# A gated scan with mixture-of-experts: expert weights loaded on another DMA queue, and a new order of the first chunk

## The chip, the cores and the metric

One Trainium2 chip, one core. The metric is the device time of one execution in microseconds; lower is better. TensorE does the matmuls, VectorE and ScalarE the elementwise work, POOL (GpSimd) issues indirect transfers from its own queue, and SP (SyncE) issues plain transfers from another.

## The reference

A gated scan over 4 sequences of 5056 tokens with 256 channels makes h; then every token is given to one of 8 experts, greedily in the order of its logits, at most 2528 tokens to each; each expert is a two-layer network.

```python
sig = 1.0 / (1.0 + np.exp(-f_logit))
f = lower_bound + (1.0 - lower_bound) * sig
h = f[:, t] * h + (1.0 - f[:, t]) * x[:, t]        # for every t; y[:, t] = h
logits = y.reshape(N, 256) @ w_gate                 # N = 20224, 8 experts
...                                                 # greedy: best logit first, cap N // 8
out[mask] = np.maximum(y[mask] @ w1[e], 0.0) @ w2[e]   # w1[e] 256 x 1024, w2[e] 1024 x 256
```

## The kernel before, in words

Up to about 165 us the kernel runs the scan, chunk by chunk, and writes the rows of h to a DRAM buffer, `hbuf`; SP issues the loads and these stores. A search over thresholds (functions `search`, `assign`, `compact`) then finds the expert that fills first, its tokens, and the row numbers of these tokens. The order in which experts come is known only at run time, so the index of the weights in use, the tile `wi`, is computed by VectorE.

From there the function `moe` runs expert after expert. An expert k has 20 blocks of 128 tokens, in chunks of up to four blocks; expert 0's first chunk has two. A chunk c has eight steps j, one for each 128 columns of the hidden layer. Each float32 operand is split into a high part in fp32r and a low part, the remainder, and each product is three matmuls: high by high, high by low, low by high.

- `load_w` (line 1050) puts the loads of expert k's weights, w1 in two halves of 512 KB and w2, at the head of the list `issues`; each is an indirect transfer on POOL that reads its row numbers from `wi`. `issue` (1039) pops from that list; in the main loop one transfer is issued per step, each waiting for the evacuation named last in `gate`. For expert 0, w2 comes in two halves, which lines 1406 to 1412 place on POOL behind the first chunk's gathers.
- `split` (1074) cuts the raw weights into eight pieces: 0 to 3 are w1, of 512 columns (pieces 0 and 1 serve steps 0 to 3 for the two halves of the contraction, 2 and 3 steps 4 to 7), 4 to 7 are w2, for two steps each. `high` writes a piece's high part on ScalarE (tiles w1h, w2s), `low` its low part on VectorE (w1l, w2s). For expert 0 the list `RAMP` (1071) says which pieces are done at each tick of `sp0`, four ticks before the first step and one after the matmuls of each step.
- `gather` (1122) lists the indirect loads of a block's rows (tile xg); `trans` (1168) transposes them on TensorE, and ScalarE and VectorE write the high and low parts xh and xl.
- `first` (1198) is one step of the first layer: six matmuls into a bank of the pool `pws` (three buffers, tile pw), which ScalarE evacuates to hh and VectorE to hl. These evacuations are not emitted at once but kept as `posts`; `flush` (1153) emits those that a model of the engines' time holds for ready, and with an argument all those up to that step.
- `second` (1263) is one step of the second layer, into tile py. `first_lag` (1431) says how many steps of the second layer have been emitted by the end of steps 3, 4 and 5; afterwards it is two steps behind.
- `tick` (1440) emits background work: the routing of later experts, the rest of the row numbers, and the split of the next expert's weights. As long as `sp0` is not done it does nothing but `flush`.

The order on TensorE, VectorE and ScalarE is the order of emission; the queues of POOL and SP are ordered by the framework. Filler matmuls (tile bz) run on TensorE while it waits for the search.

```python
    for i in range(len(todo) + LAG):
        step = i
        flush(i - 2 if i < len(todo) else i)
        ...
            first(k, c, j)
            if not sp0.done:
                flush()
            sp0.tick(True)
            tick()
        ...
        while made < first_lag.get(i, i - LAG + 1):
            second(*todo[made])
```

Of the kernel before, what the change touches and what calls it, by code (L numbers as in the profile page):

```python
# [1002 lines left out]
def moe(ctx, tc, g):  # L1003
    pace = g["pace"]
    nc = Paced(tc.nc, pace)
# [42 lines left out]
        return st  # L1048

    def load_w(k, layers=(1, 2)):  # L1050
        def load(dst, src, n):
            return lambda: nc.gpsimd.indirect_dma_start(out=dst, out_offset=None, in_=src,
                                                        in_offset=off(WI[k][:, n:n + 1]))
        rows = []
        r1 = r2 = None
        if 1 in layers:
            r1 = wraw.tile([P, 2, F], F32, name="r1")
            rows = [load(r1[:, 0], w1v, 0), load(r1[:, 1], w1v, 1)]
        if 2 in layers:
            r2 = wraw2.tile([P, FB, D], F32, name="r2")  # L1060
        if 2 not in layers:
            pass
        elif k:
            rows.append(load(r2.rearrange("p j d -> p (j d)"), w2v, 2))
        else:
            rows += [load(r2[:, s * FB // 2:(s + 1) * FB // 2].rearrange("p j d -> p (j d)"), w2u, 3 + s)
                     for s in range(2)]
        issues[:0] = [(("w", k), x) for x in rows]
        RAW[k] = r1 or RAW[k][0], r2

    RAMP = [((0, 1), (0,)), ((2,), (1,)), ((3,), (2,)), ((), (3,)), ((4,), ()), ((5,), (4,)), ((6,), (5,)),
            ((7,), (6,)), ((), (7,))]

    def split(k):
        if k:
            issue(upto=lambda what: what == ("w", k))
        r1, r2 = RAW[k]
        w1h = wsp.tile([P, 2, FB, P], F32R, name="w1h")
        w1l = wsp.tile([P, 2, FB, P], F32R, name="w1l")
        w2s = wsp.tile([P, FB, 2, 2, P], F32R, name="w2s")  # L1080
        WS[k] = w1h, w1l, w2s
        pieces = []
        for j0, h in ((0, 0), (0, 1), (4, 0), (4, 1)):
            src = r1[:, h].rearrange("p (q j) -> p j q", j=FB)[:, j0:j0 + 4]
            pieces.append((src, w1h[:, h, j0:j0 + 4], w1l[:, h, j0:j0 + 4], omlb[:, h:h + 1]))
        for j0 in range(0, FB, 2):
            src = r2[:, j0:j0 + 2].rearrange("p j (b a) -> p j a b", a=2)
            pieces.append((src, w2s[:, j0:j0 + 2, :, 0], w2s[:, j0:j0 + 2, :, 1], None))
        def high(n):
            src, hi, lo, scale = pieces[n]  # L1090
            if scale is None:
                nc.scalar.activation(hi, src, AF.Copy)
            else:
                nc.scalar.activation(hi, src, AF.Identity, scale=scale)

        def low(n):
            src, hi, lo, scale = pieces[n]
            if scale is None:
                v.tensor_sub(lo, src, hi.bitcast(F32))
            else:  # L1100
                v.scalar_tensor_tensor(lo, src, scale, hi.bitcast(F32), op0=OP.mult, op1=OP.subtract)

        steps = RAMP if k == 0 else [((n,), (n - 1,)) for n in range(len(pieces) + 1)]
        for i, (hs, ls) in enumerate(steps):
            prog[k]["left"] = len(steps) - i
            for n in hs:
                if n < len(pieces):
                    high(n)
            for n in ls:
                if n >= 0:  # L1110
                    low(n)
            yield 'ACT',

    def tiles(k, c):
        b, n = CHUNKS[k][c]
# [49 lines left out]
    def woven(t):  # L1165
        return t.rearrange("p a b -> p b a")

    def trans(k, c, h, now=False):
        ns = tiles(k, c)
        w, m = sum(ns), 2 if len(ns) <= 2 else 1  # L1170
        if h == 0:
            issue(upto=lambda what: what == ("g", k, c))
            XS[k, c] = (xp.tile([P, 2, 512], F32R, name="xh"), xp.tile([P, 2, 512], F32R, name="xl"))
        elif m == 2:
            return
        xh, xl = (turn2(t)[:, h:h + m, :, :w // 2] for t in XS[k, c])
        if now:
            def part(q):
                pt = pws.tile([P, 512], F32R, name="pw")
                pt = pt[:, :2 * P].rearrange("p (m w) -> p m w", m=2)  # L1180
                for i in range(2):
                    nc.tensor.transpose(pt[:, i], XG[k, c][:, q, i * P:(i + 1) * P], ident_r)
                pt = pairs(pt.bitcast(F32))
                qh, ql = (t[:, :, :, q * P // 2:(q + 1) * P // 2] for t in (xh, xl))
                up = post("ACT", (pt,), lambda: nc.scalar.activation(qh, pt, AF.Copy), None, now)
                post("DVE", (xh,), lambda: v.tensor_tensor(ql, pt, qh.bitcast(F32), op=OP.subtract), up, now)
                g["busy"](g["WARM"][q], g["RA"])
            return [part(q) for q in range(2)]
        pt = pws.tile([P, 512], F32R, name="pw").rearrange("p (m w) -> p m w", m=m)
        for q, n in enumerate(ns):  # L1190
            for i in range(m):
                nc.tensor.transpose(pt[:, i, q * P:q * P + n], XG[k, c][:n, q, (h + i) * P:(h + i + 1) * P],
                                    ident_r[:n, :n])
        pt = pairs(pt.bitcast(F32)[:, :, :w])
        up = post("ACT", (pt,), lambda: nc.scalar.activation(xh, pt, AF.Copy), None, now)
        return post("DVE", (xh,), lambda: v.tensor_tensor(xl, pt, xh.bitcast(F32), op=OP.subtract), up, now)
# [191 lines left out]

    main.until(lambda: have(0, "wi"))
    load_w(0, (1,))  # L1390
    issue(2)
    main.until(lambda: 0 in comp)
    for _ in g["kept"]:
        pass
# [4 lines left out]
    gp = ctx.enter_context(tc.tile_pool(name="gp", bufs=3))  # L1399
    wraw2 = ctx.enter_context(tc.tile_pool(name="wraw2", bufs=1))  # L1400
    load_w(0, (2,))
    wsp = ctx.enter_context(tc.tile_pool(name="wsp", bufs=2))
    xp = ctx.enter_context(tc.tile_pool(name="xp", bufs=2))
    hp = ctx.enter_context(tc.tile_pool(name="hp", bufs=FB))
    yp = ctx.enter_context(tc.tile_pool(name="yp", bufs=YB))
    halves = [issues.pop(0)[1] for _ in range(2)]
    gather(0, 0)
    rows = issue(99)
    for half in halves:
        tc.add_manual_dep(half().ins, rows.ins.name,  # L1410
                          mybir.DependencyInfo(mybir.DependencyClass.NoSync, mybir.DependencyReason.SCHED_ONLY),
                          reason="rows first")
    gather(0, 1, (0, 2))
    issue(99)
    comp[0].tick(True)
    comp[0].tick(True)
    sp0 = Bg(split(0))
    sp0.tick(True)
    gather(0, 1, (2, 4))
    gather(0, 2, (0, 1))  # L1420
    issue(99)
    sp0.tick(True)
    trans(0, 0, 0, True)
    sp0.tick(True)
    sp0.tick(True)
    sp = None
    todo = [(k, c, j) for k in range(E) for c in range(len(CHUNKS[k])) for j in range(FB)]
    starts = {kk: n for n, (kk, cc, jj) in enumerate(todo) if (cc, jj) == (0, 0)}
    order = [(k, c) for k in range(E) for c in range(len(CHUNKS[k]))]
    gathers = order[2:]  # L1430
    first_lag = {3: 0, 4: 1, 5: 2}
    made = 0
    LAG = 3
    wn = 1
# [4 lines left out]

    def tick():  # L1440
        nonlocal sp, wn
        if not sp0.done:
            return flush()
        if not any(rows_due(q) and comp[q].tick() for q in (k, k + 1)):
            main.tick()
        flush()
        for q in (k, k + 1, k + 2):
            if q in comp and not comp[q].done:
                comp[q].tick()
        if sp is None:  # L1450
            if wn == k + 1 and wn < E and have(wn, "wi"):
                load_w(wn)
                sp = Bg(split(wn), WAITS)
                sp.wait = WAITW
                wn += 1
        elif not sp.done:

            sp.tick(within=max(0, starts[k + 1] - i - 1) * 6 / prog[k + 1].get("left", 9))
# [4 lines that stand above are left out]
        if i < len(todo):  # L1463
            k, c, j = todo[i]
            if (c, j) == (0, 0) and k:
                assert wn == k + 1
                sp.until(lambda: sp.done)
                sp = None
            first(k, c, j)
            if not sp0.done:  # L1470
                flush()
            sp0.tick(True)
            tick()
            NS = len(CHUNKS[k])
            if gathers:

                kk, cc = gathers[0]
                ahead = order.index((kk, cc)) - order.index((k, c))
                if ahead == 1 and j >= 1 or ahead == 2 and j >= (2 if (k, c) == (0, 0) else 0) and have(
                        kk, "ids", sum(CHUNKS[kk][cc])):  # L1480
                    gather(kk, cc, (1, 4) if (kk, cc) == (0, 2) else None, soon=ahead == 1 or c == len(CHUNKS[k]) - 2 and j > 0)
                    gathers.pop(0)
            at = T0 if k < 2 and c in (0, NS - 1) else TJ
            nxt = order.index((k, c)) + 1
            if j in at and nxt < len(order):
                trans(*order[nxt], at.index(j))
# [35 lines left out]
```

## Time and profile before

| | |
|---|---|
| median of 3 runs | 1106.17 us (1104.99 to 1108.45) |
| the profiled execution | 1104.47 us, of which the span of instructions is 1102.7 us |
| granted clock of TensorE | 0.999 of full speed |
| busy, of the span | TensorE 98%, VectorE 73%, ScalarE 48%, POOL 40% |
| DMA | 121.76 MB, 58.22 on POOL's queue and 62.14 on SP's |
| chain that ended last | TensorE 80% |

All times in the profile count from the start of the span. PE is TensorE, PEld its loading of weights, DVE is VectorE, ACT is ScalarE; a q behind the name means its queue of instructions. In a timeline a row gives the start, the length, the engine, the operation with its output and inputs, their shapes, and how many such instructions the row merges; in brackets stand the engine's idle time before it and what ended it. The tile r stands for r1 and r2, the raw weights, and also for a small tile of the routing; the operation tells them apart. L109 is a helper through which most operations pass.

### The profile page before, as it was taken

The numbers are of one execution on the slowest core, as the hardware profiler recorded it, in microseconds if no ns is written. First come the engines' busy times: TensorE is split into PE (matmuls) and PEld (weight loads), VectorE is DVE, ScalarE is ACT, GpSimd is POOL, SyncE is SP. The second block draws the span as 40 slices with busy tenths as digits, with TensorE's granted clock in tenths as the row PEclk, the third lists the DMA queues.
The fourth block names the chain that finished last, engine by engine and source line by source line (L and its number), as shares of the span: only waits on it lengthen the run. The fifth ranks groups of instructions, "written<-read, shape, count | busy, mean of one in ns | idle before, by whom it ended". The sixth has DMA issues, their size and how long they took to land.

```text
span 1102.7 us, 21642 instructions
## 1 busy us (share of the span) xinstructions
PE 1084.4 (98%) x8230; PEld 959.9 (87%) x8230; DVE 803.4 (73%) x2048; ACT 533.6 (48%) x1223; POOL 446.0 (40%) x428
## 2 busy tenths in 40 slices
PE   8999998999999999999999999999999999999998
PEld 6888787999988898888888888888888888898897
DVE  7999878878877896789778877887787664334333
ACT  7999775332733454245424642264226573323322
POOL 6787404332533343344333333433343433333332
PEclk9999999999999999999999999999999999999999
DMA  9999894112111311131113111311113221111110
GB/s 372 410 399 376 318 362 140 54 38 96 63 48 44 114 50 43 43 119 58 44 44 114 48 45 46 111 57 44 48 57 109 96 73 50 49 49 52 48 48 38
DMA packets 36493, 121.76 MB, mean 110 GB/s; under 512 B 7714, under 2 KB 7716, under 8 KB 35492
## 3 DMA queue, kind: packets, MB, share of 16 engines
q0 software_dynamic: 18960, 58.22, 15.6%
q1 hardware_dynamic: 17424, 62.14, 14.6%
q8 instruction: 65, 1.06, 0.4%
q14 instruction: 40, 0.33, 0.1%
q10 hardware_dynamic: 4, 0.00, 0.0%
HBM read 78.91 MB, written 41.42 MB: 109 GB/s over the span
## 4 chain that ended last, share of the span: by engine, by line
PE 80%; issue 1%; DMA 1%; DVE 1%; POOL 0%; ACT 0%; POOLq 0%; ACTq 0%
PE pw L109 38%; PE py L109 37%; PE rt L109 4%; DMA r<-in_moe_w_dram,wi 1%; POOL out_dram L109 0%; POOL r L109 0%; DVE hl L109 0%; DVE w2s L109 0%; ACT y L109 0%; POOLq L1518 0%; DVE w1l L109 0%; ACT hh L109 0%; DVE asg L109 0%; DVE y L109 0%; DVE g L109 0%
## 5 line engine op out<-in xcount | busy, mean ns | idle before, releaser
L109 PE MATMUL py<-w2s,hh 128*128 128x512 f32 (+3 forms) x1448 | 453.4, 366 | 0.0
L109 ACT ACTIVATE hh<-pw 128x512 fp32r<-128x512 f32 (+3 forms) x336 | 192.0, 572 | 436.5 <-PE pw L109 399.0
L109 PE MATMUL py<-w2s,hl 128*128 128x256 f32 (+1 forms) x1280 | 349.6, 273 | 0.0
L109 DVE SCALAR_TENSOR_TENSOR hl<-pw,hh 128x512 fp32r<-128x512 f32 (+3 forms) x336 | 219.4, 655 | 128.0 <-ACT hh L109 126.9
L109 PEld LDWEIGHTS py<-w2s,hh 128*128 128x128 f32 (+1 forms) x1448 | 261.8, 188 | 25.9
L109 POOL DMA_INDIRECT out_dram<-y,ids x160 | 161.9, 1012 | 274.1 <-ACT hh L109 145.4
L109 POOL DMA_INDIRECT xg<-hbuf,gid x160 | 161.3, 1008 | 271.1 <-ACT hh L109 216.5
L109 PE MATMUL pw<-xh,w1h 128*128 128x512 f32 (+3 forms) x672 | 247.4, 370 | 2.6 <-DVE hl L109 1.6
L109 PE MATMUL pw<-xh,w1l 128*128 128x512 f32 (+3 forms) x672 | 248.5, 372 | 0.0
L109 PE MATMUL pw<-xl,w1h 128*128 128x512 f32 (+3 forms) x672 | 248.4, 372 | 0.0
L109 PEld LDWEIGHTS py<-w2s,hl 128*128 128x128 f32 (+1 forms) x1280 | 243.6, 190 | 4.2
L109 PEld LDWEIGHTS pw<-xh,w1h 128*128 128x128 f32 x672 | 127.0, 190 | 18.3 <-DVE hl L109 1.8
L109 PEld LDWEIGHTS pw<-xh,w1l 128*128 128x128 f32 x672 | 127.0, 190 | 13.1
L109 PEld LDWEIGHTS pw<-xl,w1h 128*128 128x128 f32 x672 | 127.7, 191 | 6.8
L109 POOL TENSOR_TENSOR xl<-fl,xl 128x1024 f32<-128x1024 f32 (+2 forms) x39 | 91.3, 2348 | 27.6 <-ACT lg L109 5.4
L109 DVE TENSOR_TENSOR_SCAN gk<-fg,gk,pb 128x512 f32<-128x512 f32 (+3 forms) x68 | 81.6, 1241 | 8.9 <-PE pb L109 6.3
L109 ACT ACTIVATE y<-py 128x256 f32<-128x256 f32 (+2 forms) x151 | 52.7, 409 | 71.3 <-PE py L109 68.1
L109 DVE TENSOR_TENSOR y<-py,y 128x256 f32<-128x256 f32 (+1 forms) x139 | 52.8, 419 | 41.9 <-ACT y L109 41.7
L109 ACT ACTIVATE junk<-rt,r 128x158 bf16<-128x158 f32 x155 | 59.1, 394 | 18.3 <-DVE R L109 12.7
L109 ACT ACTIVATE fg<-pf,nomlb 128x512 f32<-128x512 f32 (+1 forms) x80 | 54.2, 697 | 7.6 <-DVE gk L109 3.9
L109 DVE TENSOR_TENSOR xl<-pw,xh 128x512 fp32r<-128x512 f32 (+3 forms) x81 | 54.1, 669 | 0.2 <-ACT xh L109 0.2
L109 PEld LDWEIGHTS <-MK 128*128 128x128 bf16 x1141 | 37.1, 98 | 13.8 <-issue 6.2
(224 smaller groups left out, 1275.4 us busy)
## 6 DMA issues: line engine op xcount, KB each, us to landing
fl<-in_f_logit_dram SPq DMA_DIRECT2D x39, 512.0 KB, 7.3
xl<-in_x_dram SPq DMA_DIRECT2D x39, 512.0 KB, 6.6
hbuf<-hr SPq DMA_DIRECT2D x39, 512.0 KB, 4.7
xg<-hbuf,gid POOLq DMA_INDIRECT x160, 2.7
out_dram<-y,ids POOLq DMA_INDIRECT x160, 2.4
r<-in_moe_w_dram,wi POOLq DMA_INDIRECT x25, 4.9
fl<-in_f_logit_dram SPq DMA_DIRECT2D x1, 256.0 KB, 9.5
xl<-in_x_dram SPq DMA_DIRECT2D x1, 256.0 KB, 8.0
```

What stands on the lines that cost most here:

```text
L109: r = self.pace.last[self.name] = f(*args, **kw)
```

## The change

The indirect loads of the weights on POOL go, but for w1 of expert 0. In their place SP reads one element of `wi` into a register and issues a plain transfer at that address; w2 comes in two halves for every expert. For expert 0 these two halves are issued as soon as the tile's buffer exists, with no order behind the gathers. `RAMP` goes: pieces 0, 1 and 2 are made before the first chunk's transposes, piece 3 in two halves, one between the two blocks' xh and one after, and the others by the table `ramp`, each behind a `flush(i - 1)`, so that the last step's evacuations stand ahead of the piece. `tick` does only `flush` up to step 6, and the first step of the second layer is emitted in step 3 in place of step 4.

```diff
     def load_w(k, layers=(1, 2)):
-        def load(dst, src, n):
-            return lambda: nc.gpsimd.indirect_dma_start(out=dst, out_offset=None, in_=src,
-                                                        in_offset=off(WI[k][:, n:n + 1]))
+        def load(dst, src, col, top, a=slice(None)):
+            def emit():
+                if k == 0 and src is w1v:
+                    return nc.gpsimd.indirect_dma_start(out=dst, out_offset=None, in_=w1v,
+                                                        in_offset=off(WI[k][:, col:col + 1]))
+                row = nc.sync.value_load(WI[k][0:1, col:col + 1], min_val=0, max_val=top)
+                return nc.sync.dma_start(dst, src[bass.ds(row, P), a])
+            return emit
...
+            m = FB // 2
+            rows += [load(r2[:, s * m:(s + 1) * m].rearrange("p j d -> p (j d)"), w2v, 2, (E - 1) * P,
+                          slice(s * m * D, (s + 1) * m * D)) for s in range(2)]
...
-    RAMP = [((0, 1), (0,)), ((2,), (1,)), ((3,), (2,)), ((), (3,)), ((4,), ()), ((5,), (4,)), ((6,), (5,)),
-            ((7,), (6,)), ((), (7,))]
...
                 g["busy"](g["WARM"][q], g["RA"])
+                if q == 0:
+                    between()
...
     load_w(0, (2,))
+    issue(99)
...
-    halves = [issues.pop(0)[1] for _ in range(2)]
     gather(0, 0)
-    rows = issue(99)
-    for half in halves:
-        tc.add_manual_dep(half().ins, rows.ins.name,
...
+    issue(99)
...
-    sp0.tick(True)
-    trans(0, 0, 0, True)
-    sp0.tick(True)
-    sp0.tick(True)
+    high, low = split(0)
+    for n in range(2):
+        high(n)
+        low(n)
+    high(2)
+    trans(0, 0, 0, True, lambda: high(3, slice(0, 2)))
+    high(3, slice(2, 4))
+    low(2)
+    ramp = {1: (4, 4), 2: (None, 3), 3: (5, 5), 5: (6, 6), 6: (7, 7)}
...
-    first_lag = {3: 0, 4: 1, 5: 2}
+    first_lag = {3: 1, 4: 1, 5: 2}
...
-        if not sp0.done:
+        if i <= max(ramp):
             return flush()
...
-            if not sp0.done:
-                flush()
-            sp0.tick(True)
+            if i <= max(ramp):
+                flush(i - 1)
+                hi, lo = ramp.get(i, (None, None))
+                if hi is not None:
+                    high(hi)
+                if lo is not None:
+                    low(lo)
             tick()
```

## Rows read from the trace of the kernel before

**Rows 1.** Page, part 1: busy time by engine, whole span

```profile
PE 1084.4 (98%) x8230; PEld 959.9 (87%) x8230; DVE 803.4 (73%) x2048; ACT 533.6 (48%) x1223; POOL 446.0 (40%) x428
```

**Rows 2.** Windows by stretch: busy us by engine, clock, DMA share, GB/s

```profile
core 0: us, PE busy (x) PEld busy (x) DVE busy (x) ACT busy (x) POOL busy (x), PEclk, DMA share, GB/s
168.00:170.00 2.00, 1.99 (x19) 1.51 (x17) 1.78 (x9) 0.00 (x0) 1.69 (x2) 1.00 0.28 53
170.00:172.00 2.00, 1.91 (x23) 1.51 (x21) 1.79 (x11) 0.51 (x3) 0.36 (x2) 1.00 0.84 262
172.00:174.00 2.00, 2.00 (x33) 1.99 (x31) 1.44 (x12) 1.46 (x3) 0.95 (x1) 1.00 0.60 211
...
180.00:182.00 2.00, 0.38 (x4) 0.22 (x3) 1.67 (x4) 2.00 (x5) 1.39 (x3) 1.00 0.76 258
...
184.00:186.00 2.00, 1.37 (x15) 1.15 (x13) 0.91 (x2) 2.00 (x5) 0.96 (x2) 1.00 0.27 82
186.00:188.00 2.00, 1.51 (x14) 1.32 (x12) 1.97 (x9) 1.13 (x5) 0.00 (x0) 1.00 0.19 55
188.00:190.00 2.00, 1.77 (x16) 1.75 (x16) 1.83 (x9) 1.60 (x8) 0.00 (x0) 1.00 0.00 0
190.00:192.00 2.00, 1.32 (x13) 1.12 (x12) 1.97 (x8) 0.00 (x0) 0.00 (x0) 1.00 0.00 0
192.00:200.00 8.00, 8.00 (x54) 7.05 (x53) 6.59 (x17) 5.01 (x17) 3.04 (x4) 1.00 0.19 52
200.00:220.00 20.00, 20.00 (x157) 18.58 (x157) 16.33 (x38) 6.76 (x17) 7.51 (x8) 1.00 0.16 51
280.00:300.00 20.00, 19.62 (x170) 18.83 (x169) 18.42 (x42) 15.36 (x41) 11.92 (x11) 1.00 0.20 71
```

**Rows 3.** Timeline, all engines, 174 to 185 us (start, us, engine, operation)

```profile
174.81 2.41 ACT L109 ACTIVATE w1h<-r,omlb 128x512 fp32r<-128x512 f32 x2 [1.34 <-DMA r<-in_moe_w_dram,wi]
175.12 2.24 DVE L109 SCALAR_TENSOR_TENSOR w1l<-r,omlb,w1h 128x512 fp32r<-128x512 f32 x2
...
177.12 0.63 ACT L109 ACTIVATE xh<-pw 128x256 fp32r<-128x256 f32 x2
...
177.80 0.49 PE L109 MATMUL pw<-xh,w1h 128*128 128x256 f32 x2 [0.29 <-ACT xh L109]
...
180.00 0.67 ACT L109 ACTIVATE w2s<-r 128x512 fp32r<-128x512 f32 x1 [1.10 <-DMA r<-in_moe_w_dram,wi]
...
180.70 0.69 DVE L109 TENSOR_TENSOR w2s<-r,w2s 128x512 fp32r<-128x512 f32 x1 [0.27 <-ACT w2s L109]
...
181.31 1.24 DVE L109 SCALAR_TENSOR_TENSOR hl<-pw,hh 128x256 fp32r<-128x256 f32 x3
...
181.78 0.49 PE L109 MATMUL pw<-xh,w1h 128*128 128x256 f32 x2 [1.62 <-DVE hl L109]
...
184.00 0.79 ACT L109 ACTIVATE w2s<-r 128x512 fp32r<-128x512 f32 x1 [1.97 <-DMA r<-in_moe_w_dram,wi]
```

**Rows 4.** Timeline, POOL, issues of expert 0's weights (start, us, engine, operation)

```profile
167.54 1.19 POOL L109 DMA_INDIRECT r<-in_moe_w_dram,wi  x1 [2.07 <-DVE MS L109]
...
175.32 1.73 POOL L109 DMA_INDIRECT r<-in_moe_w_dram,wi  x1 [0.30 <-issue]
177.35 0.94 POOL L109 DMA_INDIRECT r<-in_moe_w_dram,wi  x1 [0.30 <-DVE w1l L109]
```

**Rows 5.** Timeline, VectorE: the index of the weights

```profile
166.39 0.22 DVE L109 SCALAR_TENSOR_TENSOR wi<-wk,sc,wb 128x5 int32<-128x5 f32 x1
```

**Rows 6.** Timeline, SP: its last issue

```profile
166.01 0.32 SPq L831 DMA_DIRECT2D hbuf<-hr  x1
```

**Rows 7.** DMA issues, 165 to 169 us: KB of one, us to landing

```profile
hbuf<-hr SPq DMA_DIRECT2D x1, 512.0 KB, 2.9
```

**Rows 8.** Timeline, POOL: last gather of the third chunk

```profile
197.15 0.95 POOL L109 DMA_INDIRECT xg<-hbuf,gid  x1 [1.28 <-ACT hh L109]
```

**Rows 9.** Timeline, weight loads of TensorE: transposes of the third chunk

```profile
200.06 0.52 PEld L109 LDWEIGHTS pw<-identr,xg 128*128 128x128 f32 x4
```

More of the change, by code (lines that the diff above doesn't have):

```diff
@@ L1057, in load_w @@
             r1 = wraw.tile([P, 2, F], F32, name="r1")
-            rows = [load(r1[:, 0], w1v, 0), load(r1[:, 1], w1v, 1)]
+            rows = [load(r1[:, h], w1v, h, (E - 1) * D + h * P) for h in range(2)]
         if 2 in layers:
             r2 = wraw2.tile([P, FB, D], F32, name="r2")
[L1061 to L1067, printed above, removed]
+            m = FB // 2
+            rows += [load(r2[:, s * m:(s + 1) * m].rearrange("p j d -> p (j d)"), w2v, 2, (E - 1) * P,
+                          slice(s * m * D, (s + 1) * m * D)) for s in range(2)]
         issues[:0] = [(("w", k), x) for x in rows]
         RAW[k] = r1 or RAW[k][0], r2
-    RAMP = [((0, 1), (0,)), ((2,), (1,)), ((3,), (2,)), ((), (3,)), ((4,), ()), ((5,), (4,)), ((6,), (5,)),
-            ((7,), (6,)), ((), (7,))]
     def split(k):
-        if k:
-            issue(upto=lambda what: what == ("w", k))
+        issue(upto=lambda what: what == ("w", k))
         r1, r2 = RAW[k]
@@ L1088, in split, with high @@
             pieces.append((src, w2s[:, j0:j0 + 2, :, 0], w2s[:, j0:j0 + 2, :, 1], None))
-        def high(n):
-            src, hi, lo, scale = pieces[n]
+        def high(n, a=slice(None)):
+            src, hi = (x[:, a] for x in pieces[n][:2])
+            scale = pieces[n][3]
             if scale is None:
@@ L1101, in low, with steps @@
                 v.scalar_tensor_tensor(lo, src, scale, hi.bitcast(F32), op0=OP.mult, op1=OP.subtract)
[L1103 to L1106, printed above, removed]
+        if k == 0:
+            return high, low
+        def steps():
+            for n in range(len(pieces) + 1):
+                prog[k]["left"] = len(pieces) + 1 - n
                 if n < len(pieces):
                     high(n)
[L1109 to L1112, printed above, removed]
+                if n:
+                    low(n - 1)
+                yield 'ACT',
+        return steps()
     def tiles(k, c):
@@ L1166, in woven, with trans @@
         return t.rearrange("p a b -> p b a")
-    def trans(k, c, h, now=False):
+    def trans(k, c, h, now=False, between=None):
         ns = tiles(k, c)
@@ L1390, in moe @@
     load_w(0, (1,))
-    issue(2)
+    issue(99)
     main.until(lambda: 0 in comp)
@@ L1405, in moe @@
     yp = ctx.enter_context(tc.tile_pool(name="yp", bufs=YB))
-    halves = [issues.pop(0)[1] for _ in range(2)]
     gather(0, 0)
-    rows = issue(99)
-    for half in halves:
-        tc.add_manual_dep(half().ins, rows.ins.name,
-                          mybir.DependencyInfo(mybir.DependencyClass.NoSync, mybir.DependencyReason.SCHED_ONLY),
-                          reason="rows first")
+    issue(99)
     gather(0, 1, (0, 2))
@@ L1416, in moe @@
     comp[0].tick(True)
-    sp0 = Bg(split(0))
-    sp0.tick(True)
     gather(0, 1, (2, 4))
@@ L1469, in moe @@
             first(k, c, j)
-            if not sp0.done:
-                flush()
-            sp0.tick(True)
+            if i <= max(ramp):
[5 more added lines that the diff above has]
+                    low(lo)
             tick()
```

## The prediction

> **What bounds the kernel now.** I read the page first: TensorE is busy 1084.4 us of a span of 1102.7 [rows 1]. So 18 us at most stand beside matmuls, and everything the change touches lies in the change-over from the routing search to expert 0 and at the later loads of weights. The windows by stretch say where TensorE stood still [rows 2]: 1.62 us in 180 to 182, 0.63 in 184 to 186, 0.49, 0.23 and 0.68 in the next three, together 3.65 us. From 192 on it is full, 8.00 of 8 and 20.00 of 20; of the 45 stretches of 20 us from 200 to 1100 the costliest but the last is 280 to 300, where expert 1's weights are split, with 0.38 us idle. The reader is to see that later loads have almost nothing to give, and that this is a change to some 14 us after 177.8.
>
> The timeline says what ended those waits [rows 3]. The first expert matmul starts at 177.80, behind ScalarE, which had waited 1.34 us for the second half of w1, made two weight pieces (2.41 us) and then both halves of xh (0.63). At 180.15 TensorE has three steps done and no free bank; it waits 1.62 us for the hl of step 0. VectorE could not make it, since ScalarE's hh stood behind a piece of w2 that waited for its transfer until 180.00. At 184.00 the same happens with the second half of w2 (1.97 us idle). Both transfers were issued late, at 175.32 and 177.35, behind w1 and two gathers on POOL [rows 4]; their index was written at 166.39 [rows 5].
>
> **The change, part by part.** Sums are made against the profiled execution, 1104.47 us with a span of 1102.7; the median of the three runs, 1106.17, stands 1.70 us above it.
>
> *w2 of expert 0 on SP.* It takes two issues (1.73 and 0.94 us) out of POOL's order [rows 4] and puts two register loads and two transfers behind SP's last store, whose issue at 166.01 took 0.32 us [rows 6]. No row shows a register load. Below it is bounded by that issue, 0.32; above by POOL's issue of an indexed load, 1.73, which also reads its index. I take 1.0, between them. Then the first issue ends at 166.6 + 1.0 + 0.3 = 167.9 and the second at 169.2. A 512 KB transfer on SP's queue landed in 2.9 us when the queue ran dry [rows 7]; doubled for company, the halves land by 173.7 and 175.0. Before, they landed at 180.0 and 184.0, so even a register load of 4 us would keep both ahead of need. The gathers that follow on POOL move up by up to 2.7 us; I count nothing for that, since the waits of the ramp end with hl or xl and none with a gather's landing.
>
> *Evacuations ahead of pieces.* With w2 there and hh ordered before the piece, the 3.65 us lose their cause, but VectorE becomes the next wait. From the last xl to step 2's hl it owes two w1l pieces (2 x 1.12), one low half of w2 (0.69) and three hl (3 x 0.41) [rows 3]: 4.1 us. TensorE has meanwhile, beside the end of step 0, steps 1 to 3, half of step 4 and one group of the second layer: four and a half groups of six matmuls at 0.7 us (177.80 to 180.16 held three, with their start-up): 3.2. I leave 0.9 us of stalls standing: a gain of 2.75, with 0 and 3.65 as ends.
>
> *Half a piece between the two xh.* The third step's piece is 1.2 us on ScalarE, so half of it is 0.6, and it now stands before the second xh, which the first matmul needs since it takes both tiles. ScalarE has no gap there (174.81 to 177.75 is one chain of pieces and xh [rows 3]), so +0.6, all on the path, which is the upper end; the lower is 0, if w1 comes so early that the second gather is what is waited for.
>
> *w1's second half in company.* The DMA share was 0.28, 0.84 and 0.60 in the three stretches from 168 to 174 [rows 2]; 262 GB/s at 0.84 is 312 GB/s at full share, so the room left is 1.28 x 2 us x 312 = 0.80 MB, and w2 brings 1.05 MB. What doesn't fit, 0.25 MB, is 0.8 us of all engines; w1 bears part of it: +0.5 taken. Ends: 0, and 1.05/0.312 = 3.4 us if all of w2 goes first. The Trainium skill (DMA: Bandwidth & Descriptors, section "Issuing engines are not separate DMA queues") says that transfers issued from different engines run on the same 16 engines and interleave, and that a second issuing engine saves only the time of issuing; by that rule alone the sum would lose the 2.75 us and keep the rest, +1.2. The trace disagrees in one thing: the late issue here was not its own cost but its place behind waits on POOL [rows 4].
>
> *Routing work put off.* The step's background tick now does nothing up to step 6, where the old order let it start at step 5. So the routing work that filled VectorE in 186 to 192 beside hl and xl (5.77 us busy [rows 2]; I put the routing at half, 3 us) moves behind the ramp. Cover: VectorE has 1.41 us free in 192 to 200 and 3.67 in the next 20 [rows 2]. If it is gone, the third chunk's gathers are late: the last was issued at 197.15 [rows 8], and its rows are transposed at 200.06 [rows 9], 2.9 us on. Ends 0 and 1.5; taken +0.3, near the covered end.
>
> *Weights of experts 1 to 7 on SP.* Three issues each leave POOL (40% busy [rows 1], no bound), four come to SP, which does nothing else then; they keep their order behind the per-step gate. One more slot of that gate is used per expert; the forced issues ahead of a transpose make up for it at no cost, and without that one late gather is a wait of at most a step. TensorE idles 0.38 us at 280 to 300 [rows 2]: -0.2 taken, ends 0 and -0.38.
>
> Sum: -2.75 + 0.6 + 0.5 + 0.3 - 0.2 = **-1.55 us**: 1102.9 against 1104.47, and 1104.6 against the median.
>
> TensorE will idle up to 2 us before its first expert matmul; it idled 1.62 at 180 to 182 with a granted clock of 1.00, the 2.4 GHz level [rows 2], so I add nothing.
>
> **The rivals.**
> *w1 behind w2 (slower).* If SP's transfers take the engines first, w1's second half lands 3.4 us late: -2.75 + 0.6 + 3.4 + 0.3 - 0.2 = +1.35, 1107.5. It decides from a delay of 0.5 + 1.55 = 2.05 us. For it: SP's issue can be out before w1's, at 167.54 [rows 4]; against it: share 0.28 in 168 to 170. Chance 0.15. The rule of the Trainium skill named above (DMA: Bandwidth & Descriptors, "Issuing engines are not separate DMA queues") points this way.
> *Given back.* The put-off routing work holds up evacuations one step later: 1.4 of the 3.65 us fell in 186 to 192 with VectorE busy 5.77 of 6 us [rows 2]. If these return and the gathers are late too, +0.3 becomes 1.4 + 0.5 = 1.9: 1106.2. Against it: VectorE's slack from 192 on. Chance 0.13.
> *All of it.* w1 as before, the half piece in a gap, no stalls left: -3.65 - 0.38 = -4.0, 1102.1. For it: w2 can flow before w1 does; against it: VectorE's 4.1 us. Chance 0.15.
> *It doesn't do what it says.* Register load and address take so long that w2 lands no earlier than 180. Then only the new order counts: step 0's hh no longer stands behind the transfer but step 1's does, so of the 1.62 one hl of 0.41 stays and 1.2 go, and 0.6 comes: 1105.6. Chance 0.05.
> *The forecast*, a gain of 0.5 to 3.3 us: 0.52.
>
> **How the numbers follow.** A measurement of this kernel can tell a change of about 0.3%, 3.3 us, from none. Only "all of it" passes that on the fast side: 0.15. On the slow side it takes w1 over 5 us late: 0.05. Within: 0.80. The range runs from "all of it", 1102.1 less a little for the scatter of runs, to the slower rival's 1107.5: 1101.9 to 1107.6.
>
> **What would show it.** Right: SP issues w2 before 170, ScalarE's pieces of w2 start with no wait for a transfer, the 1.62 at 180 is gone, TensorE's full stretch, from 192 before, begins 1.3 to 2 us earlier, and 200 to 1080 stays full. The half piece is right if the first matmul starts near 178.9 rather than 177.80: 0.5 from w1, 0.6 from the order. Wrong: w1's second half lands after 176.9, or new waits of TensorE stand behind 190, at the third chunk's transposes above all; or the first matmul comes no later and nothing is left idle.

## The result and the profile after

| kernel | executions | median us | lowest to highest |
|---|---|---|---|
| before | 6 | 1107.25 | 1104.99 to 1109.31 |
| changed | 6 | 1118.97 | 1117.00 to 1121.93 |

Ratio 1.0108, interval 1.0087 to 1.0129: **slower by 11.7 us**, where 1104.6 (1101.9 to 1107.6) was forecast. The profiled execution of the changed kernel took 1121.17 us (span 1119.1), 2.2 above its median, and that of the kernel before, 1104.47, 2.8 below its own; so the profiles lie 16.4 us of span apart where the medians lie 11.7.

Where TensorE lost the time is read from the windows by stretch, first of the kernel before (columns as in [rows 2]; its stretches 200:220 and 280:300 stand there):

```profile
160.00:180.00 20.00, 17.84 (x196) 15.41 (x195) 17.02 (x64) 9.97 (x20) 8.82 (x10) 1.00 0.68 243
180.00:200.00 20.00, 16.35 (x123) 14.61 (x122) 16.12 (x46) 11.78 (x36) 7.09 (x9) 1.00 0.25 75
...
300.00:320.00 20.00, 20.00 (x137) 17.55 (x137) 16.42 (x51) 9.80 (x32) 7.96 (x8) 1.00 0.20 56
320.00:340.00 20.00, 20.00 (x164) 17.62 (x163) 14.74 (x47) 5.99 (x13) 6.78 (x7) 1.00 0.13 39
```

and of the changed kernel:

```profile
160.00:180.00 20.00, 15.06 (x174) 12.74 (x172) 14.49 (x58) 7.92 (x15) 8.73 (x12) 1.00 0.76 273
180.00:200.00 20.00, 17.14 (x119) 16.33 (x120) 15.39 (x41) 11.71 (x32) 2.40 (x2) 0.83 0.06 18
200.00:220.00 20.00, 18.67 (x131) 17.04 (x131) 16.25 (x39) 8.58 (x25) 7.25 (x7) 1.00 0.16 50
220.00:240.00 20.00, 20.00 (x188) 18.33 (x187) 13.84 (x39) 5.76 (x10) 6.70 (x7) 1.00 0.15 48
240.00:260.00 20.00, 20.00 (x187) 18.21 (x186) 14.48 (x49) 5.95 (x11) 5.92 (x6) 1.00 0.11 39
...
280.00:300.00 20.00, 19.81 (x163) 18.73 (x161) 18.68 (x46) 14.85 (x33) 5.55 (x6) 1.00 0.33 117
300.00:320.00 20.00, 17.63 (x111) 15.88 (x112) 14.66 (x43) 9.81 (x34) 8.07 (x9) 0.91 0.16 54
320.00:340.00 20.00, 19.24 (x159) 16.77 (x158) 13.35 (x42) 6.81 (x20) 6.08 (x7) 1.00 0.13 40
```

Busy time must be weighed by the granted clock: 17.14 us at 0.83 are 14.2 at full clock. So the ramp (160 to 200) lost 2.8 + 2.1 = 4.9 us, the stretch of the third chunk (200 to 220) 1.3, and 280 to 340, the start of expert 1, 59.62 - (19.81 + 17.63 x 0.91 + 19.24) = 4.5. Together 10.8; TensorE's last matmul ends 10.0 us later. The rest is behind it. There the queues drain; GpSimd's drains by the program's line (count, shortest/median/longest ns, first and last start; the longest of the three is called its last drain here), of the kernel before:

```profile
L1518 POOLq DRAIN  x3: 46/102/3604, 1098.3 to 1102.4; - x3
```

and of the changed one:

```profile
L1523 POOLq DRAIN  x3: 46/102/10042, 1108.3 to 1118.9; - x3
```

GpSimd's last drain grew from 3.6 to 10.0 us: the other 6.4 of the 16.4. By the windows no DMA traffic runs from 1111.1 us on, so for most of it no data moves.

Three causes, then, lie on the table: the ramp, the late gathers, the drain. The ramp in the timeline of the changed kernel:

```profile
167.68 1.86 SPq L1057 DMA_DIRECT2D r<-in_moe_w_dram  x2
...
176.38 2.38 ACT L109 ACTIVATE w1h<-r,omlb 128x512 fp32r<-128x512 f32 x2 [1.29 <-DMA r<-in_moe_w_dram,wi]
176.70 0.36 PE L109 MATMUL pw<-identr,xg 128*128 128x128 f32 x2 [1.63 <-DMA xg<-hbuf,gid]
...
177.84 0.34 PE L109 MATMUL pw<-identr,xg 128*128 128x128 f32 x2
...
180.82 0.38 ACT L109 ACTIVATE xh<-pw 128x256 fp32r<-128x256 f32 x1 [2.07 <-remote]
...
182.35 0.38 ACT L109 ACTIVATE xh<-pw 128x256 fp32r<-128x256 f32 x1 [0.51 <-remote]
...
182.79 0.80 PE L109 MATMUL pw<-xh,w1h 128*128 128x256 f32 x2 [4.32 <-ACT xh L109]
```

SP issued both halves of w2 by 169.5, as reckoned, and no piece of w2 waited for its transfer any more. But w1's second half reached ScalarE at 176.38 (before 174.81, [rows 3], though the index stood 0.5 us later there), and the first chunk's own rows were late as well: TensorE waited 1.63 us for them. Each xh reads the transposes of one block; the first started 3.8 us and the second 4.2 us behind the recorded end of its transposes (177.06 and 178.18), with ScalarE idle for 2.07 and 0.51 us just before them and only "remote" given as the releaser. TensorE idled 4.32 us and began at 182.79 in place of 177.80, at half its clock.

The gathers of the third chunk ([rows 8]: last at 197.15). The first of them before:

```profile
192.75 0.94 POOL L109 DMA_INDIRECT xg<-hbuf,gid  x1 [7.48 <-ACT hh L109]
```

and all three in the changed kernel, with the wait that came of it:

```profile
197.49 1.56 POOL L109 DMA_INDIRECT xg<-hbuf,gid  x1 [16.65 <-DVE tk L109]
200.48 0.94 POOL L109 DMA_INDIRECT xg<-hbuf,gid  x1 [1.42 <-ACT hh L109]
201.76 1.06 POOL L109 DMA_INDIRECT xg<-hbuf,gid  x1 [0.34 <-ACT hh L109]
...
204.77 0.36 PE L109 MATMUL pw<-identr,xg 128*128 128x128 f32 x2 [1.21 <-DMA xg<-hbuf,gid]
```

POOL stood 16.65 us until VectorE had done a step of the list (tk), where before it stood 7.48, and the transposes waited 1.21 us for the rows. The same a second time for expert 1: the end of its search (MK is cleared then), its first weight load and its first gather, before:

```profile
262.31 0.24 POOL L109 MEMSET MK<- 128x160 bf16 x1 [5.18 <-PE rt L109]
...
266.86 0.99 POOL L109 DMA_INDIRECT r<-in_moe_w_dram,wi  x1 [4.31 <-DVE wi L109]
...
285.63 1.80 POOL L109 DMA_INDIRECT xg<-hbuf,gid  x1 [0.86 <-ACT hh L109]
```

and in the changed kernel, with the waits that came of it:

```profile
271.27 0.24 POOL L109 MEMSET MK<- 128x160 bf16 x1 [7.03 <-PE rt L109]
...
276.91 4.32 SPq L1057 DMA_DIRECT2D r<-in_moe_w_dram  x4
...
293.40 1.30 POOL L109 DMA_INDIRECT xg<-hbuf,gid  x1 [8.18 <-ACT hh L109]
...
300.41 0.28 PE L109 MATMUL pw<-identr,xg 128*128 128x128 f32 x1 [0.59 <-DMA xg<-hbuf,gid]
...
302.65 0.28 PE L109 MATMUL pw<-identr,xg 128*128 128x128 f32 x1 [1.97 <-DMA xg<-hbuf,gid]
```

### The profile page after: what moved, and what is told of

Read it like the earlier page. It is cut to its first block, busy times and chain, and to the rows that moved or that the text cites. A ratio compares the mean times of both kernels' runs of the same rounds, so it can differ in the third digit from the quotient of the medians.

```text
span 1119.1 us, 21823 instructions
## 1 busy us (share of the span) xinstructions
PE 1088.8 (97%) x8230; PEld 962.8 (86%) x8230; DVE 804.0 (72%) x2048; ACT 534.2 (48%) x1224; POOL 419.6 (37%) x405
## 4 chain that ended last, share of the span: by engine, by line
PE 86%; DVE 3%; issue 3%; DMA 2%; ACT 1%; POOL 1%; another core or an unknown queue 0%; POOLq 0%; ACTq 0%
PE py L109 37%; PE pw L109 37%; PE rt L109 4%; PE pb L109 2%; PE pl L109 2%; PE pf L109 2%; PE pr L109 1%; POOL xg L109 1%; DMA xg<-hbuf,gid 1%; DMA r<-in_moe_w_dram,wi 1%; DVE gk L109 1%; DVE hl L109 0%; POOL out_dram L109 0%; DVE MK L109 0%; ACT w1h L109 0%
## 5 line engine op out<-in xcount | busy, mean ns | idle before, releaser
L109 ACT ACTIVATE xh<-pw 128x512 fp32r<-128x512 f32 (+3 forms) x81 | 47.6, 588 | 8.4 <-PE pw L109 5.7
```

The source lines that it names most:

```text
L109: r = self.pace.last[self.name] = f(*args, **kw)
```

## The experiments

There are sixteen runs, four at a time (one of them the kernel before once more), each four on one chip with the kernel before beside them; of times, only ratios are compared across groups.

### The change in three parts

A: expert 0's w2 on SP. B: experts 1 to 7 on SP. C: the new order of evacuations and pieces, with the background held back through step 6. In the loader, `sp` is SP's load at a register's address:

```
A  rows += [sp(w2 half 0), sp(w2 half 1)] if k == 0 else [load(w2)]
B  rows  = [sp(w1 half h) if k else load(w1 half h) for h in (0, 1)]; w2: sp if k else load
C  the changed kernel with load() everywhere
AC C with A's line
```

> The kernel before, with expert 0's w2 alone loaded by SP from a register address as soon as its buffer exists; later weights stay on POOL and the old order of pieces stays. Theory 1 (the early transfers on SP are what makes the first xh late): the first expert matmul starts at 181 to 183 us in place of 177.8, with ScalarE idle for 2 us or more between the third piece of w1 and the first xh, and the time is 4 to 8 us above before. Theory 2 (the new order of pieces is at fault): first expert matmul within 1 us of 177.8, the 1.62 us wait at 180 gone, time 0 to 2 us below before.

> The kernel before, with the weights of experts 1 to 7 alone loaded by SP, in four transfers each; expert 0 as before. Theory 3 (the later loads cost: one more slot of the gate makes expert 1's gathers late, and the end of the kernel grows): TensorE waits of about 3 us for gathers at 300 to 325 us, POOL's last drain near 10 us in place of 3.6, time 6 to 10 us above before. Otherwise: within 1 us of before.

> The changed kernel with all weights loaded by POOL as before; only the new order of pieces and the shorter background ticks are left. Theory 2 (the order is at fault): first expert matmul at 181 to 183 us and the third chunk's gathers after 197, as in the changed kernel, time 4 to 8 us above before. Theory 1: first expert matmul at 178 to 179, the third chunk's gathers still late, a wait of about 1.3 us there, time from 1 us below to 2 us above before.

> The changed kernel with the weights of experts 1 to 7 loaded by POOL as before; expert 0 as changed. Theories 1 and 2 both: first expert matmul at 181 to 183 us, waits at the third chunk. Theory 3: no gather waits at 300 to 325 and a last drain of 3.6 us, so the time falls from 12 us above before to 5 to 8 above.

| run | ratio to before | interval |
|---|---|---|
| A | 1.0002 | 0.9992 to 1.0011 |
| B | 1.0038 | 1.0023 to 1.0052 |
| C | 1.0109 | 1.0083 to 1.0135 |
| AC | 1.0086 | 1.0061 to 1.0112 |

C has the whole loss by itself; A is free; B costs a third of it. B and C together make 1.47%, more than the whole change, so the parts don't simply add. In C and AC TensorE waits on gathers 7.3 and 8.9 us in all, in A 1.6, in B not at all (A's 1.6 and as much of AC's stand at the first chunk, behind the early w2). That doesn't say yet which half of C it is.

No expectation had its time right. A's profile shows theory one's ramp (first expert matmul at 183.47, ScalarE idle for 3.54 us) without its 4 to 8 us. B has theory three's drain, 10.13 us, but no wait on gathers. C took 13 us more than before and AC 10, past every range named.

### The order, or the work put off

One condition decides when the background runs:

```
     def tick():
-        if i <= max(ramp):     # held through step 6
+        if i < 5:              # from step 5 on, as before
             return flush()
```

D1 has it in the changed kernel, D3 in C, D4 in AC; D2 is the kernel before with the reverse, `if i <= 6`.

> The changed kernel with one condition put back: the routing work in the background runs again from step 5 on, as before, and not from step 7; the weights' queue and the new order of the pieces stay. Theory (the routing work put off by two steps is the loss: lists late, so gathers late at the third chunk and again around expert 1): most of the 12 us come back, 1107 to 1112 us; the last gather of the third chunk is issued near 197 and not 202, expert 1's gathers near 285 to 292 and not 293 to 300, and PE's waits on gathers fall from 6 us to under 2. Rival (the new order of evacuations and pieces itself, or the weights on SP's queue): the time stays at 1115 to 1121 and only the gathers move. Second rival (the late first evacuation beside the early weight transfer is the loss): 1114 to 1118, with the first expert matmul still past 182.

> The kernel before with its routing work in the background held back through step 6 and not step 4, and nothing else changed. Theory (put-off routing is the loss): 1115 to 1121 us, gathers of the third chunk 4 to 5 us later than before (last one at 201 to 202), expert 1's gathers 7 to 9 us later, PE waits on gathers of 5 to 9 us. Rival (the order of the pieces is the loss): 1107 to 1110, waits on gathers under 2 us.

> The kernel before with the new order of evacuations and pieces of expert 0 alone: all weights stay on GpSimd's queue and the routing work runs from step 5 on as before. Theory (put-off routing is the loss): 1105 to 1110 us, which prices the order by itself at -3 to +2. Rival (the order is the loss): 1116 to 1122, as with the later routing work.

> The kernel before with the new order and expert 0's weights of layer two on SP's queue, experts 1 to 7 on GpSimd's queue, and the routing work from step 5 on as before. Theory (put-off routing is the loss, the rest of the change is worth its 1 to 2 us): 1104 to 1109. Rival (the late first evacuation that two earlier profiles with this transfer showed costs in every execution): 1111 to 1116, first expert matmul past 182. Rival (the order itself is the loss): 1115 to 1120.

| run | ratio to before | interval |
|---|---|---|
| D1 | 1.0046 | 1.0030 to 1.0063 |
| D2 | 1.0159 | 1.0138 to 1.0180 |
| D3 | 1.0007 | 0.9991 to 1.0023 |
| D4 | 1.0000 | 0.9987 to 1.0012 |

This settles it. Putting the condition back takes C from 1.0109 to 1.0007 and AC from 1.0086 to 1.0000; putting only the delay into the kernel before makes it 1.6% slower. D1 keeps 0.46%, which is B's share. So of the change's 1.08%, nothing goes to the order and expert 0's w2 (D4), 0.46% to the later weights (D1 over D4) and 0.62% to the delay (the change over D1). Expert 1's chain in the timeline of D1, whose ramp is as late as the changed kernel's (first xh at 180.84):

```profile
263.05 0.24 POOL L109 MEMSET MK<- 128x160 bf16 x1 [0.90 <-PE rt L109]
...
268.11 3.84 SPq L1057 DMA_DIRECT2D r<-in_moe_w_dram  x4
...
287.39 1.10 POOL L109 DMA_INDIRECT xg<-hbuf,gid  x1 [1.71 <-ACT hh L109]
```

All of it is 6 to 9 us earlier than after the change, from the condition alone. In D2's timeline, an old ramp with late background:

```profile
267.50 0.24 POOL L109 MEMSET MK<- 128x160 bf16 x1 [7.03 <-PE rt L109]
...
273.67 1.13 POOL L109 DMA_INDIRECT r<-in_moe_w_dram,wi  x1 [0.30 <-DVE TR L109]
...
294.79 2.22 POOL L109 DMA_INDIRECT xg<-hbuf,gid  x1 [5.89 <-ACT hh L109]
```

Against the profile before, D2 is +5.2 us at the end of the search, +6.8 at the weights and +9.2 at expert 1's first gather; between the changed kernel and D1 the same three are 8.2, 8.8 and 6.0. So the whole chain is late, but not by one amount. D1's expectation had 1107 to 1112; it came out at 1113.2, since what B costs, 4 to 5 us, I had not added. D2 at 1124.75 went past its 1121; its profile shows, beside 7.5 us of waits on gathers, 3.1 on the routing's own junk and 1.3 on w2s.

The same delay costs 1.0% in C, 0.9% in AC and 0.6% in the changed kernel. The rest of the run behind 340 us tells why, of C:

```profile
340.00:1080.00 740.00, 735.67 (x4841) 649.82 (x4837) 518.36 (x1398) 310.37 (x743) 278.64 (x281) 1.00 0.19 63
```

and of the changed kernel:

```profile
340.00:1080.00 740.00, 739.78 (x4839) 654.63 (x4839) 519.70 (x1390) 310.89 (x742) 261.56 (x266) 1.00 0.19 64
```

TensorE idles 4.3 us there in C (4.2 in AC, 4.4 in D2), 2.7 of them in waits on gathers in C and AC, and 0.2 in the changed kernel. The three have the later experts' weights on GpSimd's queue, the changed kernel has them on SP's, and there the delay costs next to nothing more once expert 1 has started. So in the changed kernel part B also saves some 4 us of the delay. That the emptier queue of GpSimd does this is read from four profiles and not tested by itself.

### How much delay it bears

E3 is the kernel before with `if i <= 5` (one step late), E2 with `if i < 3` (two steps early), F1 is D4 with `if i < 6`.

> The kernel before with the routing work in the background held back one step longer (from step 6 on; before, from 5 on; with both steps, from 7 on, it took 1124.75 us, 16 more). Theory (each late step shifts the lists and so the gathers of the third chunk and of expert 1, whose slack is under 8 us): between the two, 1112 to 1119 us, with PE waits on gathers between none and 7.5 us. Rival (a cliff at the second step, the first is free): 1107 to 1110 and no waits on gathers.

> The kernel before with the routing work in the background let in two steps earlier, from step 3. Theory (before, the lists come just in time, so more time ahead of them buys nothing, while VectorE's ramp gets fuller): 1107 to 1111 us. Rival (the lists are still a little late before, and the later starts of expert 1 are paid by it): 1102 to 1106.

> The kernel with the new order, expert 0's layer two on SP's queue, the other experts on GpSimd's (equal to before when the routing work runs from step 5, ratio 1.000), with that work held back one step, to run from step 6. Theory (the slack of expert 1's search is between one and two steps, whatever the order of the pieces): ratio 0.999 to 1.003 and expert 1's weight loads near 263 to 269 us. Rival (the new order has used some of that slack, so that the first late step costs already): 1.004 to 1.010, weight loads of expert 1 past 271.

E3 1.0000 (0.9990 to 1.0009), E2 1.0012 (0.9998 to 1.0026), F1 1.0010 (1.0000 to 1.0019). The theory in E3's expectation fell, the rival held in the time: one step late is free, two cost 1.6%, two early gain nothing. Not quite in the trace: E3's TensorE waits 1.55 us for the third chunk's rows at 203.23. But its chain of expert 1 is not late: search, weights and first gather stand at 265.63, 270.17 and 289.13, and at 265.52, 270.07 and 289.35 in E1 of the same group, whose ramp is as late and whose background starts as before. F1 has its weight load at 264.84. Why the first step is absorbed there and the second is not is not shown; it is a cliff between a start at step 6 and one at step 7, wherever the ramp's pieces stand.

### GpSimd's last drain

E1 moves expert 7 alone to SP, E4 experts 1 to 6, F3 layer two of all experts (on D4), F4 layer one of experts 1 to 7 (on the kernel before). Each is A's or B's line with another condition, as `if k == E - 1`.

> The kernel before with the weights of expert 7 alone on SP's queue (four transfers at a register's address in place of three of GpSimd's). With experts 1 to 7 there, GpSimd's last drain after the final store took 10.1 us in place of 3.6, and the whole was 0.38% slower. Theory one (what the last transfers on SP's queue leave behind lengthens the drain): drain near 10 us, 1111 to 1115 us. Theory two (the drain goes by how many transfers GpSimd's own queue has carried: 345 before, 324 with experts 1 to 7 moved, here 342): drain 3.4 to 3.6 us, 1107 to 1109.

> The counterpart: experts 1 to 6 on SP's queue, expert 7 on GpSimd's as before, 327 transfers on GpSimd's queue. Theory one (what stands last on SP's queue): drain 3.5 us, 1106 to 1109 us. Theory two (the count on GpSimd's queue): drain near 10 us, 1110 to 1114, as with experts 1 to 7.

> New order, layer two of all experts on SP's queue, layer one on GpSimd's, routing work from step 5: 336 transfers on GpSimd's queue. Theory (the last drain goes by that count and jumps between 327 and 342): a drain of 2.9 to 3.3 us and ratio 0.997 to 1.001 if the jump lies below 336; 10.6 to 11 us and 1.003 to 1.006 if above. Rival (the drain goes by transfers on SP's queue in the second half of the run, as the 14 here and the four of expert 7 do not explain alike): a value between, 5 to 8 us.

> The kernel before with layer one of experts 1 to 7 on SP's queue and layer two on GpSimd's as before: 331 transfers on GpSimd's queue. Theory (count): drain 2.8 to 3.1 us and ratio 0.997 to 1.001, or, if the jump lies above 331, 10.5 to 10.7 us and 1.003 to 1.005. Rival (the moved transfers themselves cost, whatever the drain): ratio over 1.002 with a drain under 4 us.

| run | transfers on GpSimd's queue | weights' transfers on SP's | drain us | ratio to before |
|---|---|---|---|---|
| before | 345 | 0 | 3.60 | |
| D4 | 343 | 2 | 3.49 | 1.0000 (0.9987 to 1.0012) |
| E1 | 342 | 4 | 3.46 | 0.9991 (0.9982 to 1.0001) |
| F3 | 336 | 16 | 3.17 | 1.0006 (0.9997 to 1.0016) |
| F4 | 331 | 14 | 2.91 | 0.9998 (0.9988 to 1.0007) |
| E4 | 327 | 24 | 10.37 | 1.0041 (1.0021 to 1.0062) |
| B | 324 | 28 | 10.13 | 1.0038 (1.0023 to 1.0052) |
| changed | 322 | 30 | 10.04 | 1.0108 (1.0087 to 1.0129) |

On both sides of the jump, the lines of F4 and E4:

```profile
L1519 POOLq DRAIN  x3: 46/102/2914, 1098.2 to 1101.7; - x3
L1519 POOLq DRAIN  x3: 46/102/10367, 1102.7 to 1113.6; - x3
```

The drain follows the count: it falls by 0.03 to 0.08 us with each transfer less on GpSimd's queue, and between 331 and 327 jumps up by 7.5. Runs of one count agree: 3.59 to 3.61 in six profiles at 345, 3.49 to 3.50 in four at 343, 10.04 in both at 322 (a seventh at 345, F2, showed 3.93). It doesn't matter which weights are moved: E4 leaves expert 7 on GpSimd and has the long drain, E1 and F3 put expert 7's or the last w2 on SP and have the short one. F3, with more transfers on SP's queue than F4 and fewer bytes on GpSimd's (49.83 against 50.88 MB), has the longer drain, so at the short level it goes by GpSimd's count and by neither of these. For the jump that isn't settled: it also lies between 16 and 24 transfers on SP's queue, and every moved transfer takes the same 144 packets with it, so that count and packets can't be told apart. F4's 14 moved transfers cost nothing in the whole; what B costs stands in the drain. E1 and E4 took longer than their expectations had it, as did the kernel before beside them (1111.35); drain and ratio came out as theory two had them. None of these beats the kernel before by what can be measured.

### The late first evacuation

> The kernel before, unchanged, for one profile on this chip. Question: is the late first evacuation of a chunk (TensorE's transposes recorded 3 to 4 us ahead of the release of ScalarE, first expert matmul past 181) a thing of the early transfers on SP's queue or of any execution? Theory one (of any): it appears here in some form, first expert matmul past 180, clock 0.997. Theory two (of SP's transfers): first expert matmul at 177.5 to 178.5 as in the profile before, clock 0.999.

The kernel before, one execution: 1104.67 us, first expert matmul at 177.10. In the group with F1, F3 and F4 no kernel had the 3 to 4 us between transposes and xh, SP's transfers or not (F3: first xh at 178.79, first matmul 180.12, clock 1.00). In the group with E1 to E4 it stood in kernels that leave expert 0's w2 on GpSimd, as in E3's timeline (the second block's transposes and xh):

```profile
176.35 0.37 PE L109 MATMUL pw<-identr,xg 128*128 128x128 f32 x2
...
181.14 0.38 ACT L109 ACTIVATE xh<-pw 128x256 fp32r<-128x256 f32 x1 [2.59 <-remote]
...
181.57 0.79 PE L109 MATMUL pw<-xh,w1h 128*128 128x256 f32 x2 [4.56 <-issue]
```

F2 alone came out as theory two had it; E3 and its group put theory two, that it belongs to SP's early transfers, out. Of theory one this holds, that it comes and goes with executions or chips. The kernel before had medians of 1104.9 to 1111.35 in the four groups, the last in E's group, at a clock of 0.997 there. A's profile had it too (1111.69), its nine other executions took 1107.9 to 1109.9. What delays the release is not shown. The Trainium skill (Perfetto Trace Analysis, section "Tensor Engine Instruction (MATMUL, LD_WEIGHTS)") says that the end of a matmul in a profile is computed and not observed; that a reader can start up to 4.4 us behind that computed end is seen in these traces, and whether the matmuls themselves ended so late is not.

## Why the prediction was wrong

**Routing work put off: +0.3, ends 0 and 1.5.** This is the step that failed. Measured: 1.0109 - 1.0007 = 1.0% or 11 us in C, 0.86% in AC, 0.62% or 7 us in the changed kernel itself (1.0108 - 1.0046). The prediction took the work as an amount, 3 us of VectorE's time, and looked for VectorE's free time to cover it. But it is a chain: each tick does one stage, and search, weights' index, list and gather stand behind each other. With the ticks of two steps not given all of it was late, free VectorE or not: from 220 to 260 VectorE of the changed kernel is free for 11.7 of 40 us, and the search still ends at 271.27 where D1, with the same ramp, has 263.05. It was also followed to the third chunk alone, 2.9 us of cover, and not to the next user of the chain, expert 1, 100 us on, where most of the loss fell. "200 to 1080 stays full" was the sign named, and it broke at 204.77 and 300.41.

**Weights of experts 1 to 7: -0.2.** The sign failed: +0.38% to +0.46%, 4 to 5 us. The gain on the way exists: B's TensorE is full from 280 to 300, where that of before idles 0.38 us. The last drain, which no step of the prediction looked at, takes 6.5.

**Register load 1.0, issues at 167.9 and 169.2, w2 in time.** Right. The changed kernel's 30 register loads took 0.07 to 0.79 us, median 0.27. The Trainium skill (DMA: Bandwidth & Descriptors, section "Latency and other measured facts") gives a `tensor_load`, which is the trace's name for the instruction, a floor of about 600 ns; the trace differs and decides.

**w1's second half in company: +0.5, ends 0 and 3.4.** Under-sized. ScalarE's work on that half, the second xh and the first expert matmul in B, whose expert 0 is loaded and ordered as before:

```profile
173.79 2.38 ACT L109 ACTIVATE w1h<-r,omlb 128x512 fp32r<-128x512 f32 x2 [0.68 <-DMA r<-in_moe_w_dram,wi]
...
178.20 0.38 ACT L109 ACTIVATE xh<-pw 128x256 fp32r<-128x256 f32 x1 [1.12 <-PE pw L109]
...
178.63 0.49 PE L109 MATMUL pw<-xh,w1h 128*128 128x256 f32 x2 [1.62 <-ACT xh L109]
```

and in F3, with the same index time (165.91):

```profile
176.52 2.38 ACT L109 ACTIVATE w1h<-r,omlb 128x512 fp32r<-128x512 f32 x2 [1.11 <-DMA r<-in_moe_w_dram,wi]
...
178.79 0.36 ACT L109 ACTIVATE xh<-pw 128x256 fp32r<-128x256 f32 x1
...
179.70 0.37 ACT L109 ACTIVATE xh<-pw 128x256 fp32r<-128x256 f32 x1
...
180.12 0.49 PE L109 MATMUL pw<-xh,w1h 128*128 128x256 f32 x2 [1.52 <-ACT xh L109]
```

That is 2.7 us later for w2 on SP (2.0 in F1, 2.6 in the changed kernel), near the upper end and about or past the 2.05 us from which the prediction let its rival "w1 behind w2" decide. That is the rule of the Trainium skill on shared engines (DMA: Bandwidth & Descriptors, section "Issuing engines are not separate DMA queues") which the prediction cited; the trace agrees with it. The gathers are in that company too: the first chunk's transposes waited 1.63 us for rows in the changed kernel and 1.71 in F3, where the prediction had no wait of the ramp end with a gather's landing.

**Half a piece between the two xh: +0.6.** Right in size, where nothing else holds the second xh: F3's two xh start 0.91 us apart and F1's 0.90, without a wait, against about 0.3 in the kernel before, whose two together take 0.63. In D3 the second xh came at 178.18, after 1.10 us of waiting for its transposes, and the first matmul at 178.61; but B, with the old order, shows the same at 178.20 and 178.63, so that wait is the late release in a small form and not the half piece.

**Stalls of the ramp: -2.75, ends 0 and 3.65.** Over-sized. F3's windows, with w2 there in time and the 1.62 us wait gone:

```profile
184.00:186.00 2.00, 1.44 (x13) 1.22 (x12) 1.97 (x8) 0.61 (x2) 0.00 (x0) 1.00 0.00 0
186.00:188.00 2.00, 1.79 (x19) 1.70 (x18) 1.97 (x7) 1.98 (x9) 0.00 (x0) 1.00 0.01 4
188.00:190.00 2.00, 0.81 (x9) 0.62 (x7) 1.83 (x11) 1.38 (x3) 0.00 (x0) 1.00 0.00 0
190.00:192.00 2.00, 2.00 (x20) 2.00 (x20) 2.00 (x7) 0.71 (x2) 0.95 (x1) 1.00 0.00 0
192.00:200.00 8.00, 7.57 (x53) 6.96 (x52) 7.58 (x17) 4.27 (x16) 3.58 (x3) 1.00 0.22 60
```

Behind its first matmul TensorE still idles 0.56 + 0.21 + 1.19 + 0.43 = 2.39 us, against 3.65 before (3.37 in F2): a gain of 1.0 to 1.3. VectorE is busy 7.77 of the 8 us from 184. VectorE takes the wait's place, as the prediction said, but with 2.4 us and not with 0.9 left: its 4.1 us counted only xl, w1l, w2s and hl up to step 2, and the stretch goes on with pieces, routing and xl. In D3, the new order with w2 still on GpSimd, 3.11 us are left up to 192.

**The clock.** The prediction had TensorE idle up to 2 us before its first expert matmul and added nothing for the clock, since 1.62 us of idle time had left it at 1.00. In F3, after 1.52 us, that held; in the changed kernel's profile TensorE idled 4.32 us and ran at 0.50, the 1.2 GHz level, from 182 to 186.

The ramp's terms would thus have summed to a loss of about 2 us (F3's busy time from 160 to 200 is 32.60, F2's 34.65). D4 and F3 end level all the same. F3 has no idle time at 260 to 300, where F2 has 0.92, and a drain 0.76 shorter, together 1.7; its span is 0.3 longer. So the two profiles agree, and what made up for the ramp is not what the prediction counted on. The rival "given back" had the right direction, and its price was 1.6 where the put-off work cost 7.

## What to carry to other kernels

When a background chain is paced by ticks, cost a tick not given as a delay of the whole chain and follow it to every later user, with the slack at each. Free time on the engine is no cover for a chain of dependent stages; how much delay the chain bears has to be measured, as here one step and not two. And look at the tail of the program, behind the last matmul, whenever transfers change queues.

## What the runs showed of the hardware

GpSimd's last drain follows how many transfers its queue has carried in the whole run: from 3.60 us at 345 down to 2.91 at 331, and 10.37 at 327 down to 10.04 at 322. In the changed kernel, whose drain is 10.04, no DMA traffic runs in the last 8 us of the span. Whether the jump goes by that count, or by what SP's queue carried instead (16 against 24 of the moved transfers), and what it is, is not known.

Two transfers of 512 KB on SP's queue beside those on GpSimd's made the second half of w1 usable 2.0 to 2.7 us later (173.79 in B, 175.81 in F1, 176.52 in F3).

ScalarE started on TensorE's transposes up to 4.4 us behind their recorded end in some executions on some chips, whichever queue carried the weights. In the changed kernel's profile TensorE idled 4.32 us over it, and its granted clock was 0.50 for the stretch behind (182 to 186), its 1.2 GHz level. A's profile, which had it, took 3.0 us more than A's median; whether A's other executions had it is not known.
